# V in one transfer from ScalarE's queue, diagonal sums behind the masks, G's third band on VectorE: one planned attention-and-MLP kernel

## The chip, the cores and the metric

The kernel runs on 1 core of a Trainium2 chip. The metric is the device time of one execution in microseconds; the time before is 406.51 us, the median of 3 runs (405.24 to 407.18).

## The reference

Two stages, cut to what matters. Batch B is 4, heads H 8, positions S 768, head width D 48, model width 384, rank R 32, MLP width 1536.

```python
for t in range(S):
    cur = einsum('bhd,bhe->bhde', u * k[t], v[t])
    y[t] = einsum('bhd,bhde->bhe', r[t], state + cur)
    state = w * state + einsum('bhd,bhe->bhde', k[t], v[t])
x = y as (B, S, H * D)
xt = x.transpose(0, 2, 1)
u = x + (xt @ U @ V).transpose(0, 2, 1)
out = u + relu(u @ w_ch1) @ w_ch2
```

## The kernel before

**Attention in chunks.** Each batch's 768 positions are six chunks of 128 (`n` counts them over all batches; 0 to 5 are batch 0). A chunk's r, k and v come by DMA (`a_load`, L732, 192 KB each). TensorE turns r and k (`a_tr`, L849, tiles `ptr` and `ptk`); VectorE or ScalarE scales or copies the result (`rT` L858, `kT` L858 or L860). Scores go to `pab` (L881), updates of the running state to `pav` and `pst` (L895). VectorE masks the scores (`am`, L1018) and adds the state (`S`, L1057, L1059); ScalarE decays it for the next chunk (`SW`, L1067, four instructions). The chunk's output is summed in `pav` (L914, L918).

**The diagonal.** `a_dv` (L798) multiplies r by k on GpSimd, `a_dv_u` (L811) multiplies by u, `a_dg` (L818) sums over the head width on VectorE into `dg`, and ScalarE then multiplies v by `dg`, head by head, into `dv` (L822, eight instructions). `a_x` (L1027, VectorE) adds `dv` to the output sum and gives `x`. The next chunk's output sum may only begin when that read of `pav` is over.

**The low-rank step.** U and V, like the MLP weights, come as 64-bit words and are joined to 32 bits by ScalarE (L620, L633) and VectorE (L616, L623, L626). Six products with `x` (L1132) give G in three column groups of 32 rows. `c_g` writes G in three bands of rows: the rounded value (`high`, L1156, ScalarE), the rest (`low`, L1164, VectorE) and the rounded value again (`again_`, L1160, ScalarE). Then TensorE adds V times G to the turned x (`c_xu`, tiles `pu`, `uT`), and the MLP of batch 0 begins (`m_1`, `m_2`, L414). From there on TensorE interleaves the MLP of one batch with the attention of the next.

**What sets the order.** Every operation is recorded with a key (its rank) and a modelled duration; `Plan.schedule` then fixes the order on each engine, and the program is written in that order. Each engine, and each DMA queue, works through its list in order. SyncE (SP) issues nearly all DMAs. Each DMA signals one of eight semaphores, DMAHW0 to DMAHW7, in turn over all DMAs of the program, and a DMA that uses one of them again first waits until the earlier DMA of that semaphore has landed. The plan's model has no such wait.

**Lines that the change touches.** `unit` has `load`, which issues a weight's transfers (L595), and `weight_units` lists them; V is four transfers of 32 rows (L676), not a "big one" that counts among those in flight. `sel` (L1517) is the selection matrix with which `v_split` spreads V's pieces on TensorE. `prepare` records a chunk's diagonal sum of batch 0 (L1548) ahead of its visit, and `c_g` the bands.

Of the kernel before, what the change touches and what calls it, by code (L numbers as in the profile page):

```python
# [354 lines left out]
def rwkv_moe(ctx: ExitStack, tc: tile.TileContext, r, k, v, w, u, U, V, w1, w2, out):  # L355
    nc = tc.nc
# [51 lines left out]
    def f32(ap):  # L408
        return ap.bitcast(F32)
# [162 lines left out]
    def unit(name, shape, parts, split):  # L572

        P_ = shape[0]
        n = 1
        for s_ in shape[1:]:
            n *= s_
        raw = big([128, 2 * n], I32, f"raw_{name}") if wide else big([128, n], F32, f"raw_{name}")

        def view(ap):  # L580
            return ap if len(shape) == 2 else ap.rearrange("p (a c) -> p a c", a=shape[1])

        loaded = [(raw, i) for i in range(len(parts))]

        def load(mark=None):
            big_one = len(parts) == 1 and name != "u"
            before = landing[-FLYING] if big_one and len(landing) >= FLYING else None
            mine = []
            if big_one:
                landing.append((mine, Buf(const, [1, 1], F32, None, 1, f"landed_{name}")))  # L590
            for i, (p0, ap) in enumerate(parts):
                runs = 1 if len(ap.shape) == 2 else ap.shape[1]

                def start(q, p0=p0, ap=ap):
                    mine.append(q.dma_start(view(raw.t[p0:p0 + ap.shape[0]]), ap.bitcast(I32) if wide else ap))  # L595
                    if before:
                        tc.add_manual_dep(mine[0].ins, before[0][0].ins.name,
                                          mybir.DependencyInfo(mybir.DependencyClass.Sync, mybir.DependencyReason.DATA),
                                          reason="no more of them at a time")
                dma(start, [(raw, i)] + ([landing[-1][1]] if big_one else []), ([before[1]] if before else []) + ([mark] if mark else []),  # L600
                    ap.shape[0] * runs, (8 if wide else 4) * n // runs, ns=370, late=LATE + 1500 * (name == "v") + SLACK * (big_one and len(landing) <= 2 * EARLY))

        def word(i):
            return raw.t[:P_].rearrange("p (n two) -> p two n", two=2)[:, i]

        def byte():
            return raw.t[:P_].bitcast(U8).rearrange("p (n e) -> p n e", e=8)[:, :, 3]

        def fl():
            return view(word(0).bitcast(F32) if wide else raw.t[:P_])  # L610

        def on_dve_byte():
            return nc.vector.tensor_scalar(word(0), byte(), 2.0 ** -5, 7.0, ALU.mult, ALU.min)  # L616

        def on_act_byte():

            nc.scalar.activation(word(0), byte(), AF.Copy, scale=7.49 / 255)  # L620

        def sign():
            return nc.vector.scalar_tensor_tensor(word(0), word(1), -2 ** 31, word(0), ALU.bitwise_and, ALU.bitwise_or)  # L623

        def join():
            return nc.vector.scalar_tensor_tensor(word(0), word(1), 3, word(0), ALU.logical_shift_left, ALU.bitwise_or)  # L626

        def convert():
            if wide:
                op("DVE", 100 + 0.65 * n, on_dve_byte, [(raw, "lo")], loaded, lock=True,  # L630
                   alt=[("ACT", act(n) + 100, on_act_byte, False)])
            if wide:
                on_act(n, lambda: nc.scalar.activation(word(1).bitcast(F32), word(1).bitcast(F32), AF.Copy,  # L633
                                                       scale=2.0 ** -112), [(raw, "hi")], loaded)
                mark = [pool_done] if name in ALONE else []
                op("DVE", dve(n), sign, [(raw, "lo")], [(raw, "hi")] + mark, lock=True)
                op("DVE", dve(n), join, [(raw, "lo")], [(raw, "hi")], lock=True)
            split(fl, raw)
        return load, convert

    def weight_units():
        units = []

        def split_to(d, key, name):
            t = d[key] = big([128, 2, DM], F32R, name)

            def go(fl, raw):
                def to(i):
                    return t.t[:, i] if len(fl().shape) == 2 else t.t[:, i].rearrange("p (c n) -> p c n", c=NCT)
                on_act(384, lambda: nc.scalar.copy(to(0), fl()), [(t, 0)], [raw])  # L650
                on_either(384, lambda e: e.tensor_tensor(to(1), fl(), f32(to(0)), ALU.subtract), [(t, 1)],  # L651
                          [raw, (t, 0)], only=None)
            return go

        def u_split(fl, raw):
            on_act(192, lambda: nc.scalar.copy(Uf.t, fl()), [Uf], [raw])

        def v_split(fl, raw):
            for j in range(S // DM):
                pt = bank(("tr", "sc")[j], f"pv_{j}")  # L660

                def spread(j=j, pt=pt):
                    for i in range(DM // NV):
                        c = j * (DM // NV) + i
                        whole(pt.t[:3 * R, i * NV:(i + 1) * NV],
                              lhsT=sel.t[:, c * 3 * R:(c + 1) * 3 * R], rhs=fl(),
                              start=(i == 0), stop=(i == DM // NV - 1), skip_group_check=True)
                sl = slice(j * DM, (j + 1) * DM)
                pe(715, spread, [pt], [raw, sel], k=4)
                on_act(384, lambda sl=sl, pt=pt: nc.scalar.copy(V3.t[:, sl], pt.t[:3 * R, :DM]), [(V3, j)], [pt])  # L670
                on_dve(384, lambda e, sl=sl, pt=pt: e.tensor_tensor(V3.t[2 * R:, sl], pt.t[2 * R:3 * R, :DM],
                                                                    f32(V3.t[2 * R:, sl]), ALU.subtract), [(V3, j)], [pt])

        units.append(unit("u", [128, NCH, R], [(0, U.rearrange("(c p) r -> p c r", p=128))], u_split))
        NV = S * R // 128
        units.append(unit("v", [128, NV], [(c * R, V[:, c * NV:(c + 1) * NV]) for c in range(128 // R)], v_split))  # L676
        for f in range(NFT):
            fs = slice(f * 128, (f + 1) * 128)
            units.append(unit(f"w1_{f}", [128, NCT, 128], [(0, w1[:, fs].rearrange("(c p) n -> p c n", p=128))],
                              split_to(W1, f, f"w1s_{f}")))  # L680
            units.append(unit(f"w2_{f}", [128, DM], [(0, w2[fs, :])], split_to(W2, f, f"w2s_{f}")))
        return units
# [9 lines left out]
    def front(n):  # L692

        return n < NCH
# [444 lines left out]
    def c_g(b):  # L1139
# [8 lines left out]
        if not b:  # L1148
            G = Gs[b] = wbuf([3 * R, DM], F32R, "Gs", 1, f"Gs_{b}")

            def piece(g):
                return slice(g * 128, (g + 1) * 128), pt.t[g * R:(g + 1) * R, c0:c0 + 128]

            def high(g):
                c, p = piece(g)
                nc.scalar.copy(G.t[0:R, c], p)  # L1156

            def again_(g):
                c, _ = piece(g)
                nc.scalar.copy(G.t[2 * R:3 * R, c], f32(G.t[0:R, c]))  # L1160

            def low(e, g):
                c, p = piece(g)
                e.tensor_tensor(G.t[R:2 * R, c], p, f32(G.t[0:R, c]), ALU.subtract)  # L1164
            for g in range(NCT):
                on_act(128, lambda g=g: high(g), [(G, (0, g))], [pt])
            for g in range(NCT):
                on_dve(128, lambda e, g=g: low(e, g), [(G, (1, g))] + ([g_done] if g == NCT - 1 else []), [pt, (G, (0, g)), (G, (0, NCT - 1))])
            for g in range(NCT):
                on_act(128, lambda g=g: again_(g), [(G, (2, g))], [(G, (0, g))])  # L1170
            return
        gf = wbuf([R, DM], F32, "xl", NXS, f"gf_{b}")
        for g in range(4):
# [339 lines left out]
    for _ in range(START):  # L1513
# [2 lines left out]
    at(-99, lambda: a_load(0))  # L1516
    at(-98, lambda: on_act(384, lambda: nc.scalar.copy(  # L1517
        sel.t.rearrange("p (c k r) -> p c k r", k=3, r=R),
        ident_.rearrange("p (c r) -> p c r", r=R).unsqueeze(2).broadcast_to([128, 128 // R, 3, R])), [sel], []))
    at(UB, load_u)  # L1520
    at(-97, lambda: urgent(tables))
    for n in range(1, NCH):
# [18 lines left out]
    def prepare(n, t):  # L1541
# [3 lines left out]
        elif n < NCH:  # L1545
            fs = fs[1:2] + fs[3:4] + fs[2:3] + fs[:1] + fs[4:]
        fs.append(lambda: a_dv_u(n))
        if front(n):  # L1548
            fs.append(lambda: a_dg(n))
        for i, f in enumerate(fs):  # L1550
            at(t + (0.1 if n < NCH else 0.2) * i, (lambda f=f: urgent(f)) if n < NCH else lambda f=f: behind(u_done, f))

# [7 lines left out]
    def attention(b, t0, per, lead, step):  # L1560
        n0 = b * NCH
        end0 = t0 + per * NCH
        for c in range(NCH):
# [6 lines left out]
                    at(t - 2 * lead + 0.05 + 0.1 * i, lambda i=i: urgent(lambda: keep_busy(1 - i)))  # L1570
            if c == 0:
                at(t - 1, lambda n=n: urgent(lambda: a_first(n)) if b == 0 else a_first(n))
            at(t, lambda n=n: urgent(lambda: a_visit(n)) if b == 0 else a_visit(n))
            if n >= NCH:
                at(t - 0.1, lambda n=n: behind(u_done, lambda: a_dg(n)))
# [92 lines left out]
```

## Time and profile before

| | before |
|---|---|
| median of 3 runs (lowest to highest) | 406.51 us (405.24 to 407.18) |
| the three runs in order | 407.18, 406.51, 405.24 us |
| span of the profiled execution, first to last instruction | 406.6 us |
| TensorE, VectorE, ScalarE, GpSimd busy | 394.2, 274.8, 177.2, 65.4 us |
| TensorE's granted clock, mean over the span | 0.994 |

The profiled execution's own time is known as this span; it stands 0.1 us above the median of the runs. TensorE shows 97% of the span busy, but matmuls are pipelined and their ends modelled. What one edit is worth is read from its stage: the first 44.55 us are the attention of batch 0 and G, with waits; after them TensorE is busy almost without a break.

### The profile page before, as it was taken

The page shows a single profiled execution, that of the slowest core. Times are in us where ns is not written, and L with a number is a line of the kernel's source. Part 1 is how long each engine was busy: PE and PEld are TensorE (multiplying, and loading weights), DVE is VectorE, ACT ScalarE, POOL GpSimd, SP SyncE. Part 2 cuts the span into 40 slices and gives each one's busy share as a digit, 9 for nine tenths or more (in the row PEclk, how much of TensorE's full clock was granted, in tenths as well). Part 3 has the DMA queues.
Part 4 walks back from the last instruction along what each step waited for, and adds up shares of the span by engine and source line. Part 5 has one row for each costly group of instructions (what it writes and reads, how often), then busy time and mean ns, then how long its engine had stood idle before and what let it go on. Part 6 is the DMA issues. An engine that isn't in the chain of part 4 may idle for free.

```text
span 406.6 us, 11920 instructions
## 1 busy us (share of the span) xinstructions
PE 394.2 (97%) x4928; PEld 376.1 (92%) x4928; DVE 274.8 (68%) x615; ACT 177.2 (44%) x432; POOL 65.4 (16%) x86
## 2 busy tenths in 40 slices
PE   8997999999999999999999999999999999999994
PEld 5876899999998999999999999999999999999993
DVE  7868889999999979789647678898515261221122
ACT  2795859673786324223324242222224243223320
POOL 2960120233523302011003100010001000000000
PEclk9998999999999999999999999999999999999999
DMA  9969797968967765686667755782200520001001
GB/s 143 168 153 240 139 252 154 255 111 164 260 123 146 168 168 82 117 154 127 126 108 134 145 117 78 134 155 62 60 2 2 117 60 0 2 0 58 2 0 65
DMA packets 195741, 46.27 MB, mean 114 GB/s; under 512 B 179422, under 2 KB 194144, under 8 KB 195680
## 3 DMA queue, kind: packets, MB, share of 16 engines
q1 hardware_dynamic: 194352, 44.85, 55.2%
q8 instruction: 40, 0.66, 0.7%
q10 hardware_dynamic: 1328, 0.59, 0.5%
q14 instruction: 21, 0.17, 0.1%
HBM read 37.16 MB, written 8.26 MB: 112 GB/s over the span
## 4 chain that ended last, share of the span: by engine, by line
PE 75%; SPq 8%; DMA 5%; issue 4%; DVE 3%; POOL 2%; ACT 1%; DVEq 0%; POOLq 0%
PE p L414 64%; SPq L732 4%; PE pab L881 3%; SPq L771 2%; PE pav L932 2%; SPq L595 2%; PE pav L937 2%; PE pab L895 1%; DMA ub<-ud 1%; PE pab L414 1%; DMA ldr<-in_r_dram 1%; DMA ldv<-in_v_dram 1%; DMA vsw<-in_v_dram 1%; PE pav L914 1%; PE pav L918 1%
## 5 line engine op out<-in xcount | busy, mean ns | idle before, releaser
L414 PE MATMUL p<-uTh,w1s 128*128 128x384 f32 x576 | 147.6, 337 | 0.0
L1321 ACT ACTIVATE hr<-p 128x384 f32<-128x384 f32 x96 | 47.1, 491 | 178.0 <-PE p L414 173.7
L414 PE MATMUL p<-w2s,hh 128*128 128x384 f32 x576 | 119.6, 338 | 0.1
L1323 DVE TENSOR_TENSOR hl<-hr,hh 128x384 fp32r<-128x384 f32 x83 | 46.1, 555 | 102.3 <-ACT hh L1322 99.9
L414 PEld LDWEIGHTS p<-uTh,w1s 128*128 128x128 f32 x576 | 103.5, 188 | 0.9 <-DVE w1s L651 0.3
L414 PEld LDWEIGHTS p<-w2s,hh 128*128 128x128 f32 x576 | 100.7, 188 | 1.4 <-POOL w2s L651 0.4
L414 PE MATMUL p<-uTl,w1s 128*128 128x384 f32 x288 | 96.2, 335 | 0.0
L414 PE MATMUL p<-w2s,hl 128*128 128x384 f32 x288 | 66.7, 335 | 0.0
L414 PEld LDWEIGHTS p<-uTl,w1s 128*128 128x128 f32 x288 | 54.0, 188 | 0.1
L414 PEld LDWEIGHTS p<-w2s,hl 128*128 128x128 f32 x288 | 51.3, 188 | 0.2
L1322 ACT CAST hh<-hr 128x384 fp32r<-128x384 f32 x96 | 49.2, 512 | 2.5
L822 ACT ACTIVATE dv<-ldv,dg 128x48 f32<-128x48 f32 x96 | 23.1, 322 | 6.6 <-DVE dg L818 6.5
L1323 POOL TENSOR_TENSOR hl<-hr,hh 128x384 fp32r<-128x384 f32 x13 | 13.2, 1016 | 64.0 <-PE pav L937 36.7
L1095 POOL TENSOR_TENSOR SW<-S,wm 112x192 f32<-112x192 f32 x13 | 6.6, 508 | 93.2 <-DVE S L1086 87.8
L881 PEld LDWEIGHTS pab<-rT,kT 48*64 48x64 f32 x768 | 13.6, 134 | 7.7 <-issue 3.0
L1018 DVE TENSOR_TENSOR am<-pab,mask 128x256 f32<-128x256 f32 x48 | 19.1, 413 | 1.2 <-PE pab L881 1.1
L881 PE MATMUL pab<-rT,kT 48*64 48x64 f32 x768 | 16.9, 224 | 2.4 <-DVE rT L858 2.4
L1027 DVE TENSOR_TENSOR x<-pav,dv 128x384 f32<-128x384 f32 x24 | 13.1, 548 | 6.7 <-PE pav L937 5.2
L1361 DVE TENSOR_TENSOR x<-p,x 128x384 f32<-128x384 f32 x33 | 16.3, 548 | 1.0 <-PE p L414 1.0
L818 DVE TENSOR_REDUCE dg<-dv 128x8 f32<-128x384 f32 x24 | 13.0, 540 | 2.4 <-POOL dv L811 2.3
L626 DVE SCALAR_TENSOR_TENSOR raw_w<-raw_w 128x384 int32<-128x384 int32 x24 | 13.0, 549 | 0.1
L633 ACT ACTIVATE raw_w<-raw_w 128x384 f32<-128x384 f32 x24 | 13.0, 556 | 0.0
(178 smaller groups left out, 503.0 us busy)
## 6 DMA issues: line engine op xcount, KB each, us to landing
raw_w<-in_moe_w_ch_dram SPq DMA_DIRECT2D x24, 384.0 KB, 5.0
ldv<-in_v_dram SPq DMA_DIRECT2D x24, 192.0 KB, 3.9
ldk<-in_k_dram SPq DMA_DIRECT2D x20, 192.0 KB, 4.4
ldr<-in_r_dram SPq DMA_DIRECT2D x20, 192.0 KB, 4.0
bl<-in_r_dram SPq DMA_DIRECT2D x79, 48.0 KB, 3.1
bl<-in_k_dram SPq DMA_DIRECT2D x79, 48.0 KB, 2.4
ud<-x SPq DMA_DIRECT2D x18, 192.0 KB, 3.2
ub<-ud SPq DMA_DIRECT2D x18, 192.0 KB, 3.6
```

The lines of the kernel that those rows point to most:

```text
L414: return nc.tensor.matmul(*args, **kw)
L626: return nc.vector.scalar_tensor_tensor(word(0), word(1), 3, word(0), ALU.logical_shift_left, ALU.bitwise_or)
L633: on_act(n, lambda: nc.scalar.activation(word(1).bitcast(F32), word(1).bitcast(F32), AF.Copy, scale=2.0 ** -112), [(raw, "hi")], loaded)
L732: dma(lambda q, i=i, src=src: q.dma_start(part(i)[:, :, :D], src[b, :, c * C:(c + 1) * C, :].rearrange("h p d -> p h d")), [ts[i]] if n < ...
L822: nc.scalar.activation(dv.t[:, h], v_of(n, h), AF.Copy, scale=dg.t[:, h:h + 1])
L881: return nc.tensor.matmul(pt.t[o * C2:(o + 1) * C2, q * C2:(q + 1) * C2], lhsT=kT.t[rows, q, i * C2:(i + 1) * C2], rhs=rT.t[rows, q, i * C ...
L1018: on_dve(256, lambda e: e.tensor_tensor(am.t, abs_[n][j].t[:, :SU].rearrange("p (h t) -> p h t", h=NP), mask_.unsqueeze(1).broadcast_to([1 ...
L1027: nc.vector.tensor_tensor(x.t[:, c0:c1], pav[0].t[:, c0:c1], dv.t.rearrange("p h d -> p (h d)")[:, c0:c1], ALU.add)
L1321: on_act(384, lambda: nc.scalar.activation(hr.t, pt.t[:, :TB], AF.Relu), [hr], [pt])
L1322: on_act(384, lambda: nc.scalar.copy(hh.t, hr.t), [hh], [hr])
L1323: on_either(384, lambda e: e.tensor_tensor(hl.t, hr.t, f32(hh.t), ALU.subtract), [hl], [hr, hh], only=None)
L1361: on_dve(384, lambda e, x=x, pt=pt: e.tensor_tensor(x.t, pt.t[:, :DM], x.t, ALU.add), [x], [pt])
```

## The change

V is loaded by one transfer of 128 rows of 384 words, issued from ScalarE's queue, and `sel` selects every fourth row instead of a block of 32. Batch 0's diagonal sums are recorded just ahead of the chunk's visit, so that they rank behind the masks of that chunk. G's third band is copied by VectorE, group by group behind the second band, and the second band no longer names the last group of the first as what it waits for. V, now a single part, still isn't one of the big transfers that are counted in flight.

```diff
         def load(mark=None):
-            big_one = len(parts) == 1 and name != "u"
+            big_one = name not in ("u", "v")
...
-                    ap.shape[0] * runs, (8 if wide else 4) * n // runs, ns=370, late=LATE + 1500 * (name == "v") + SLACK * (big_one and len(landing) <= 2 * EARLY))
+                    ap.shape[0] * runs, (8 if wide else 4) * n // runs, ns=370, eng="ACT" if name == "v" else "SP", late=LATE + 1500 * (name == "v") + SLACK * (big_one and len(landing) <= 2 * EARLY))
...
-        units.append(unit("v", [128, NV], [(c * R, V[:, c * NV:(c + 1) * NV]) for c in range(128 // R)], v_split))
+        units.append(unit("v", [128, NV], [(0, V.rearrange("r (c n) -> (r c) n", n=NV))], v_split))
...
-            def again_(g):
+            def again_(e, g):
                 c, _ = piece(g)
-                nc.scalar.copy(G.t[2 * R:3 * R, c], f32(G.t[0:R, c]))
+                e.tensor_copy(G.t[2 * R:3 * R, c], f32(G.t[0:R, c]))
...
             for g in range(NCT):
                 on_act(128, lambda g=g: high(g), [(G, (0, g))], [pt])
-            for g in range(NCT):
-                on_dve(128, lambda e, g=g: low(e, g), [(G, (1, g))] + ([g_done] if g == NCT - 1 else []), [pt, (G, (0, g)), (G, (0, NCT - 1))])
-            for g in range(NCT):
-                on_act(128, lambda g=g: again_(g), [(G, (2, g))], [(G, (0, g))])
+                on_dve(128, lambda e, g=g: low(e, g), [(G, (1, g))] + ([g_done] if g == NCT - 1 else []), [pt, (G, (0, g))])
+                on_dve(128, lambda e, g=g: again_(e, g), [(G, (2, g))], [(G, (0, g))])
...
-        ident_.rearrange("p (c r) -> p c r", r=R).unsqueeze(2).broadcast_to([128, 128 // R, 3, R])), [sel], []))
+        ident_.rearrange("p (r c) -> p c r", r=R).unsqueeze(2).broadcast_to([128, 128 // R, 3, R])), [sel], []))
...
-        if front(n):
-            fs.append(lambda: a_dg(n))
...
+            if n < NCH:
+                at(t - 0.05, lambda n=n: urgent(lambda: a_dg(n)))
             at(t, lambda n=n: urgent(lambda: a_visit(n)) if b == 0 else a_visit(n))
```

In the order rows below a tile's number only tells two tiles of one name apart, and what stands behind "waits" are semaphores: of an engine, or DMAHWn of a DMA.

ScalarE's queue in chunks 0 and 1 (`dv_211` and `dv_278` or `dv_281` are the `dv` of chunks 0 and 1, `SW` the decayed state), before:

```order
L822 ACTIVATE dv_211<-ldv_112,dg_270 128x48 [waits DMAHW4_49,DVE_49]
L822 ACTIVATE dv_211<-ldv_112,dg_270 128x48 x7
L1067 ACTIVATE SW_325<-S_1_274,wm 112x96 [waits DVE_49]
L1067 ACTIVATE SW_325<-S_1_274,wm 112x96 x3
L822 ACTIVATE dv_278<-ldv_138,dg_344 128x48 [waits DMAHW7_49,DVE_49]
```

and now:

```order
L1067 ACTIVATE SW_276<-S_1_270,wm 112x96 [waits DVE_49]
L1067 ACTIVATE SW_276<-S_1_270,wm 112x96 x3
L595 DMA raw_v<-in_moe_V_dram 128x384 [waits DMAHW5_49]
L822 ACTIVATE dv_211<-ldv_112,dg_274 128x48 [waits DMAHW4_49,DVE_49]
L822 ACTIVATE dv_211<-ldv_112,dg_274 128x48 x7
L1067 ACTIVATE SW_360<-S_1_351,wm 112x96 [waits DVE_49]
```

The decay of chunk 0's state moved ahead of chunk 0's `dv`, and V's transfer stands between the two, with a wait for DMAHW5.

SP's queue in the change, around the load of chunk 3's v (`ldv_272`), the last DMA on DMAHW5 ahead of V's (each of these waits for the semaphore that it uses again):

```order
L732 DMA ld_128<-in_r_dram 128x8x48 [waits DMAHW4_49]
L732 DMA ldv_272<-in_v_dram 128x8x48 [waits DMAHW5_49]
L595 DMA raw_u<-in_moe_U_dram 128x6x64 [waits DMAHW6_49]
L732 DMA ldk_330<-in_k_dram 128x8x48 [waits DMAHW7_49]
L732 DMA ldr_120<-in_r_dram 128x8x48 [waits DMAHW0_49]
L732 DMA ldv_381<-in_v_dram 128x8x48 [waits DMAHW1_49]
L732 DMA ldk_419<-in_k_dram 128x8x48 [waits DMAHW2_49]
```

V's transfer waits until chunk 3's v has landed; chunk 5's k (`ldk_419`) now follows chunk 4's v (`ldv_381`) at once, where V's four transfers stood between them.

VectorE around chunk 0's x (`x_337`, now `x_358`), before:

```order
L1018 TENSOR_TENSOR am_1_323<-pab_108,mask 128x256 [waits PE_49]
L1027 TENSOR_TENSOR x_337<-pav_247,dv_211 128x384 [waits Activation_49]
L818 TENSOR_REDUCE dg_344<-dv_278 128x8 [waits Pool_49]
L1059 TENSOR_TENSOR S_0_349<-pav_90,SW_325 112x384 [waits PE_49,Activation_49]
L858 TENSOR_TENSOR kT_356<-ptk_242,tabT 112x512 [waits PE_49]
L1059 TENSOR_TENSOR S_1_388<-pst,S_0_349 112x384 [waits DVE_49]
```

and now:

```order
L1018 TENSOR_TENSOR am_1_324<-pab_108,mask 128x256 [waits PE_49]
L1059 TENSOR_TENSOR S_0_335<-pav_90,SW_276 112x384 [waits PE_49,Activation_49]
L858 TENSOR_TENSOR kT_344<-ptk_242,tabT 112x512 [waits PE_49]
L1059 TENSOR_TENSOR S_1_351<-pst,S_0_335 112x384 [waits DVE_49]
L1027 TENSOR_TENSOR x_358<-pav_247,dv_211 128x384 [waits Activation_49]
L858 TENSOR_TENSOR rT_383<-ptr_332,tabT 112x512 [waits PE_49]
L818 TENSOR_REDUCE dg_410<-dv_281 128x8 [waits Pool_49]
```

Chunk 0's x, which waits for ScalarE's `dv`, moved behind chunk 1's two state sums; chunk 2's `rT` and chunk 1's diagonal sum stand behind it.

## Rows read from the trace of the kernel before

**Rows 1.** Busy us of each engine by stage, granted clock, DMA share, GB/s.
```profile
0.00:44.55 44.55, 38.88 (x786) 31.22 (x786) 36.04 (x99) 27.99 (x97) 19.64 (x33) 0.96 0.96 178
44.55:100.00 55.45, 55.33 (x715) 53.11 (x714) 51.69 (x117) 39.16 (x93) 13.03 (x16) 1.00 0.82 181
```
**Rows 2.** The chain that ended last, in batch 0's attention: start us, us, what.
```profile
23.72 4.34 DMA ldr<-in_r_dram
...
29.34 0.97 POOL dv L811
...
40.60 0.60 PE wake L1132 x12
```
**Rows 3.** Timeline of VectorE, two places: start us, us, what [idle before, its releaser].
```profile
12.03 0.54 DVE L818 TENSOR_REDUCE dg<-dv 128x8 f32<-128x384 f32 x1
12.49 0.55 DVE L1059 TENSOR_TENSOR S<-pst,S 112x384 f32<-112x384 f32 x1
...
14.80 0.55 DVE L1027 TENSOR_TENSOR x<-pav,dv 128x384 f32<-128x384 f32 x1
...
30.33 0.55 DVE L818 TENSOR_REDUCE dg<-dv 128x8 f32<-128x384 f32 x1 [2.33 <-POOL dv L811]
```
**Rows 4.** Timeline of TensorE: chunk 5's scores.
```profile
32.75 0.69 PE L881 MATMUL pab<-rT,kT 48*64 48x64 f32 x32 [2.38 <-DVE rT L858]
```
**Rows 5.** Three stretches, columns of rows 1: chunk 0's x to chunk 5's scores, then outputs of chunks 4, 5.
```profile
14.80:32.75 17.95, 15.01 (x407) 12.72 (x405) 14.48 (x32) 16.74 (x65) 12.45 (x17) 1.00 0.78 181
33.45:36.50 3.05, 3.05 (x50) 2.73 (x49) 2.22 (x7) 1.20 (x3) 0.00 (x0) 0.50 1.05 216
37.80:39.75 1.95, 1.95 (x50) 1.78 (x49) 1.54 (x4) 0.92 (x2) 0.00 (x0) 1.00 1.06 155
```
**Rows 6.** Timeline of the queues of SP and ScalarE: DMA issues.
```profile
11.83 1.02 SPq L732 DMA_DIRECT2D ldv<-in_v_dram  x1
12.89 2.46 SPq L595 DMA_DIRECT2D raw_u<-in_moe_U_dram  x1
...
17.89 4.09 SPq L595 DMA_DIRECT2D raw_v<-in_moe_V_dram  x4
...
0.81 0.43 ACTq L732 DMA_DIRECT2D ld<-in_k_dram  x1
```
**Rows 7.** DMA issues at 10.45 and at 12.89: KB, us from issue to landing.
```profile
ld<-in_r_dram SPq DMA_DIRECT2D x1, 192.0 KB, 6.2
...
raw_u<-in_moe_U_dram SPq DMA_DIRECT2D x1, 192.0 KB, 5.2
```
**Rows 8.** Waits of SP's queue: us in total, times, longest us.
```profile
SPq L732 <- PE pab L849: 5.8, 3, 2.1
```
**Rows 9.** Timeline of ScalarE from chunk 0 to chunk 3.
```profile
12.61 1.92 ACT L822 ACTIVATE dv<-ldv,dg 128x48 f32<-128x48 f32 x8 [3.15 <-DVE dg L818]
14.43 1.16 ACT L1067 ACTIVATE SW<-S,wm 112x96 f32<-112x96 f32 x4
...
20.53 0.37 ACT L620 ACTIVATE raw_u<-raw_u 128x192 int32<-128x192 uint8 x1
20.80 0.36 ACT L633 ACTIVATE raw_u<-raw_u 128x192 f32<-128x192 f32 x1
21.07 0.56 ACT L860 COPY kT<-ptk 112x512 f32<-112x512 f32 x1
...
22.61 0.54 ACT L822 ACTIVATE dv<-ldv,dg 128x48 f32<-128x48 f32 x2
23.06 0.36 ACT L656 COPY Uf<-raw_u 128x192 f32<-128x192 f32 x1
23.32 1.46 ACT L822 ACTIVATE dv<-ldv,dg 128x48 f32<-128x48 f32 x6
```
**Rows 10.** Timeline of ScalarE and VectorE at G: third band, second band.
```profile
42.07 0.69 ACT L1160 CAST Gs<-Gs 32x128 fp32r<-32x128 f32 x3
...
42.76 0.92 DVE L1164 TENSOR_TENSOR Gs<-wake,Gs 32x128 fp32r<-32x128 f32 x3
```

## The prediction

> **What bounds the kernel now.** I read the busy time by stage first: from 44.55 us on TensorE stands still for 0.1 us in the 55 that follow, while up to 44.55 it is busy for 38.88 us only, at a mean clock of 0.96 [rows 1]. So what matters is when the first stage ends; whatever its last step, G, is late by, the end of the kernel is late by, one to one. I take that for every term below.
>
> The chain of waits then names what sets that stage's end: the load of chunk 5's r, landing at 28.06 (23.72 + 4.34), GpSimd's products for the diagonal up to 30.31, and, at its end, the products with x for G until 41.20 [rows 2]. VectorE's timeline says why GpSimd stands in that chain: a diagonal sum is in its queue ahead of work that is more urgent, and VectorE idles 2.33 us for it at 30.33 [rows 3]. TensorE's scores of chunk 5 come at 32.75 after 2.38 us of idling for VectorE's `rT` [rows 4]. What the idling costs beyond itself is in the windows: the granted clock then is 0.50 (1.2 GHz) and chunk 4's output takes 3.05 us, where chunk 5's, the same 50 matmuls, takes 1.95 at 2.4 GHz [rows 5]. That is 1.10 us; the scores and the G products on either side of it bring my estimate to 1.48 us for the whole half-clock stretch.
>
> **V's transfer on ScalarE.** SP gets rid of four issues that take 4.09 us [rows 6], so chunk 5's loads could come up to 4.1 us earlier. ScalarE gets one issue; its only load in this profile took 0.43 us there [rows 6]. But the order shows that this issue waits for a DMA semaphore, DMAHW5, last used by chunk 3's v, and that all of ScalarE's work, chunk 0's `dv` first, is queued behind it. That a queue can stand still like this is what SP's waits show: 5.8 us in three waits of up to 2.1 us [rows 8]. By the Trainium skill, "DMA: Bandwidth & Descriptors", section "Anatomy of one DMA — SWDGE (gpsimd) path", a semaphore wait is served by the issuing sequencer before the transfer is dispatched; the SP waits agree with it, and no row here shows it for ScalarE.
>
> When does chunk 3's v land? SP issues it at 11.83 [rows 6]. Its neighbour issued at 10.45 took 6.2 us, so landed at 16.65; U's, issued at 12.89, took 5.2 and landed at 18.09 [rows 7]. So v landed between the two; I take 17.4, the middle. ScalarE reaches the issue earlier. The diagonal sum, which VectorE did at 12.03 ahead of the state sum, now goes behind it, so the state sum is over at about 12.03 + 0.55 = 12.58 [rows 3]; `SW` takes 1.16 [rows 9] and ends near 13.8. Then ScalarE stands from 13.8 to 17.4, issues until 17.85, and runs chunk 0's `dv` (1.92 [rows 9]) until 19.77, where it now runs it at 12.61 to 14.53.
>
> Who waits for that: VectorE's `x` of chunk 0, at 14.80 now [rows 3], moves to about 19.85, and chunk 2's `rT` and chunk 1's diagonal sum are queued behind it. Chunk 1's output on TensorE waits for that `x` as well. TensorE will idle some 3 us there, and I expect its half-clock stretch there and not at chunk 4; it costs little, because ScalarE is later still.
>
> From chunk 0's `dv` on, ScalarE is the chain. Up to its copy of chunk 5's kT the new order gives it four `dv` (4 x 1.92), four `SW` (4 x 1.16), U's two joins (0.73), two `kT` (2 x 0.56), `Uf` (0.36), chunk 3's split `dv` (0.54 + 1.46) and two of chunk 5's (0.54): 17.07 us. Instructions overlap by about 0.10 (12.61 + 1.92 is 14.53, the next group begins at 14.43 [rows 9]); with 16 such hand-overs this is some 15.5. Waits add an estimated 1.2: 0.75 for chunk 1's diagonal sum behind the late `x`, and the rest for state sums and transposes. So the copy starts at 17.85 + 15.5 + 1.2 = 34.6, and is over at 35.2. VectorE is no later: from `x` to `rT` it has 14.48 us of work now [rows 5], less about 1.5 for the state sums and the `kT` that go ahead of `x`, plus 0.5 for U's join, as wide as a state sum: 19.85 + 13.5 = 33.3. So chunk 5's scores begin at about 35.2 in place of 32.75: **2.45 later**. The earlier loads are no use then, and the old wait for GpSimd is covered.
>
> From there to the end of the G products it is 41.20 − 32.75 = 8.45 us now; without the half-clock stretch (1.48) it is 6.95. So they end at 42.15: **+0.95 us**.
>
> **Diagonal sums behind the masks.** The same 96 `dv` and as many sums remain; nothing is added. The gain is the 2.33 us at 30.33 [rows 3], and it lies within the reckoning above: what is late next is ScalarE. With V on a queue that doesn't stall, this part would be the whole of the gain (rival 1).
>
> **G's third band.** VectorE's second band begins at 42.76, when ScalarE's third band, 0.69 us from 42.07, is over [rows 10]. So taking the third band off ScalarE shortens nothing by itself, and VectorE gets three more instructions. A copy of that shape costs ScalarE 0.23 (0.69/3), VectorE's second band 0.31 (0.92/3) [rows 10]; I take 0.31, the engine's own, for +0.92 at most. Against it, one weight join as wide as a state sum (0.55 [rows 3], some 0.47 with its overlap) that now stands ahead of the second band goes behind, and VectorE may begin as soon as the first group is rounded, not the last, for which I take another 0.25 off. Net **+0.2**, with ends of −0.5 and +0.9.
>
> **Selection.** `sel` is the same number of elements from another stride, once, long before it is needed: 0; its cover is the whole of the attention stage.
>
> **Sum.** 406.6 + 0.95 + 0.2 = **407.8 us**. The span of 406.6 stands 0.1 above the median of the runs, so nothing is added for that. This case's own range, by the landing (16.65 to 18.09, −0.75 to +0.7) and G's ends, is 406.3 to 409.2. Half a per cent, 2.0 us, is about what a measurement of this kernel can tell from no change; so this case is "same".
>
> **Rival 1: ScalarE doesn't stall.** If the landing is no condition when ScalarE comes to the issue, or the wait is held by the queue and not by the engine, `dv` begins at 13.8 + 0.43 = 14.25, `x` of chunk 0 at about 16.3, and the copy of kT ends at 14.25 + 15.5 + 1.2 + 0.55 = 31.5. Scores begin 1.3 earlier than now, the half-clock stretch is gone (1.48), G adds 0.2: 404.0. For it speaks the 0.43 us of the k load [rows 6], which nothing held up; against it that this load was ScalarE's first, with no semaphore to use again, and that SP is held by such waits [rows 8]. Chance 0.2. The Trainium skill, same page, section "Issuing engines are not separate DMA queues", says that issuing from several engines saves only the sequencer's issue time; by it the loads can gain at most the 4.09 us that SP loses, and no bandwidth, which leaves this rival at 404.0.
>
> **Rival 2, slower: the issue is expensive.** V's transfer may cost its queue what the 192 KB of U cost SP, 2.46 us [rows 6], in place of 0.43. All of it falls on ScalarE's chain: +2.0, 409.8. From 0.85 us more on that chain than I reckon the kernel is slower by 2.0, so an issue above 1.3 us decides for it. U has six runs to a row where V has one, which speaks against it; chunk loads of eight runs took 1.02 on SP [rows 6] and 0.43 on ScalarE. Chance 0.15.
>
> **Rival 3, slower: the half clock comes back.** If TensorE, with ScalarE pacing it, idles some 2.4 us ahead of chunk 5's scores as it does now [rows 4], the 1.48 us isn't given back: 409.3. Against it: the delay lies at chunk 1, and TensorE has 15.01 us of work in the 17.95 before the scores [rows 5], so the rest of its idle time should come in pieces. Chance 0.15.
>
> **How the numbers follow.** The forecast has 0.5, rival 1 0.2, rivals 2 and 3 0.15 each. Faster is rival 1: 0.2; slower are rivals 2 and 3: 0.3; same the rest: 0.5. The range reaches from rival 1 with a little of its own spread, 403.8, to rival 2, 410.0.
>
> **What would show it.** ScalarE idle from about 13.8, with V's issue at about 17.4 and chunk 0's `dv` at 17.9; `x` of chunk 0 near 19.85 with a long idle ahead of it; the clock low at chunk 1 and not at chunk 4; scores of chunk 5 near 35; G's products ending near 42.1; six alternating small VectorE instructions at G; chunk 5's r landing near 24. I am wrong if `dv` of chunk 0 begins by 14.5 (rival 1), if the issue itself takes over a microsecond (rival 2), or if the clock is 0.50 after the scores of chunk 5 (rival 3).

## The result and the profile after

| | before | after |
|---|---|---|
| median of the runs | 406.43 us (4 runs, 405.24 to 407.18) | 411.27 us (4 runs, 410.72 to 412.23) |
| ratio, 95% interval | | 1.0117 [1.0074, 1.016] |
| span of the profiled execution | 406.6 us | 409.6 us |
| TensorE's mean granted clock in it | 0.994 | 0.991 |

The kernel became 4.8 us slower. That is above the range (410.0 at most), on the side to which I had given 0.3.

The busy time by stage of the kernel after (from:to, us, then PE, PEld, DVE, ACT, POOL busy with their counts, clock, DMA share, GB/s):

```profile
0.00:44.55 44.55, 38.50 (x774) 31.00 (x774) 33.68 (x92) 26.73 (x90) 19.61 (x33) 0.92 0.96 183
44.55:100.00 55.45, 53.40 (x658) 50.95 (x657) 51.02 (x117) 39.05 (x92) 10.69 (x13) 1.00 0.75 164
20.15:26.55 6.40, 6.36 (x110) 5.60 (x114) 4.25 (x10) 4.32 (x17) 2.82 (x4) 0.50 0.76 167
```

Beside [rows 1]: in the first 44.55 us ScalarE was busy for 1.3 us less (26.73 against 27.99), the clock is 0.92, and there is a stretch of 6.4 us at 0.50. ScalarE's timeline, from chunk 0 on:

```profile
12.62 1.17 ACT L1067 ACTIVATE SW<-S,wm 112x96 f32<-112x96 f32 x4 [3.16 <-DVE S L1059]
17.18 0.36 ACTq L595 DMA_DIRECT2D raw_v<-in_moe_V_dram  x1
17.64 1.91 ACT L822 ACTIVATE dv<-ldv,dg 128x48 f32<-128x48 f32 x8 [3.85 <-DMA ldv<-in_v_dram]
...
21.23 1.91 ACT L822 ACTIVATE dv<-ldv,dg 128x48 f32<-128x48 f32 x8 [0.62 <-DVE dg L818]
...
26.19 0.58 ACT L860 COPY kT<-ptk 112x512 f32<-112x512 f32 x1 [1.46 <-PE ptk L849]
```

ScalarE is done with the decay at 13.79 and idles 3.85 us; V's issue comes at 17.18 and takes 0.36; chunk 0's `dv` begins at 17.64 instead of 12.61 [rows 9]. The row names a load of v as what ended the idling. It is chunk 3's v, for which V's issue waits: SP issued it at 11.93, and it landed 5.2 us later, at 17.13, 0.05 us before V's issue began.

```profile
11.93 2.27 SPq L732 DMA_DIRECT2D ldv<-in_v_dram  x1
```

The last of ScalarE's rows is a second wait, of 1.46 us, for transposes of TensorE (chunk 3's k). VectorE's timeline:

```profile
19.58 0.56 DVE L1027 TENSOR_TENSOR x<-pav,dv 128x384 f32<-128x384 f32 x1 [3.06 <-ACT dv L822]
...
41.92 0.55 DVE L651 TENSOR_TENSOR w1s<-raw_w,w1s 128x384 fp32r<-128x384 f32 x1
42.50 0.56 DVE L1027 TENSOR_TENSOR x<-pav,dv 128x384 f32<-128x384 f32 x1
...
44.61 0.28 DVE L1164 TENSOR_TENSOR Gs<-wake,Gs 32x128 fp32r<-32x128 f32 x1
44.92 0.22 DVE L1160 CAST Gs<-Gs 32x128 fp32r<-32x128 f32 x1
```

Chunk 0's `x` is at 19.58 instead of 14.80 [rows 3]; chunk 5's is at 42.50, behind a weight's split; the third band of G alternates with the second, and each of its copies takes 0.22. TensorE's two longest waits (us in total, times, longest), and its scores of chunk 5, the last six products with x and the first MLP product:

```profile
PE pav L914 <- DVE x L1027: 2.5, 1, 2.5
PE pab L881 <- ACT kT L860: 0.7, 1, 0.7
```

```profile
36.17 0.69 PE L881 MATMUL pab<-rT,kT 48*64 48x64 f32 x32 [0.67 <-ACT kT L860]
...
43.12 0.42 PE L1132 MATMUL wake<-x,Uf 128*32 128x128 f32 x6 [0.25 <-DVE x L1027]
...
46.93 0.59 PE L414 MATMUL p<-uTh,w1s 128*128 128x384 f32 x2
```

The scores come 3.42 us later than at 32.75 [rows 4], the first MLP product 2.38 later than at 44.55, where the second stage of [rows 1] begins. From there to the end it is 362.7 us, before it was 362.05.

### The profile page after: what moved, and what is told of

It is laid out like the page before. It is cut to its first block, busy times and chain, and to the rows that moved or that the text cites. A ratio compares the mean times of both kernels' runs of the same rounds, so it can differ in the third digit from the quotient of the medians.

```text
span 409.6 us, 11920 instructions
## 1 busy us (share of the span) xinstructions
PE 395.6 (97%) x4926; PEld 377.0 (92%) x4926; DVE 273.7 (67%) x616; ACT 183.2 (45%) x453; POOL 65.5 (16%) x84
## 4 chain that ended last, share of the span: by engine, by line
PE 65%; DVE 3%; SPq 1%; DMA 1%; issue 0%; ACT 0%; DVEq 0%; ACTq 0%
PE p L414 58%; PE pab L881 2%; PE pav L932 1%; PE pav L937 1%; PE pab L895 1%; PE pab L414 1%; SPq L771 1%; PE pab L1132 1%; DMA bl<-in_k_dram 1%; DVE raw_w L626 0%; DVE rT L840 0%; DVE hl L1321 0%; DVE raw_w L623 0%; DVE w2s L651 0%; DVE x L1359 0%
## 5 line engine op out<-in xcount | busy, mean ns | idle before, releaser
L1321 DVE TENSOR_TENSOR hl<-hr,hh 128x384 fp32r<-128x384 f32 x88 | 48.9, 555 | 102.0 <-ACT hh L1320 100.2
L822 ACT ACTIVATE dv<-ldv,dg 128x48 f32<-128x48 f32 x112 | 26.9, 322 | 11.2 <-DVE dg L818 6.2
L1321 POOL TENSOR_TENSOR hl<-hr,hh 128x384 fp32r<-128x384 f32 x8 | 8.1, 1016 | 64.8 <-PE pav L937 39.1
L1095 POOL TENSOR_TENSOR SW<-S,wm 112x192 f32<-112x192 f32 x11 | 5.6, 507 | 70.8 <-DVE S L1086 64.6
L811 POOL TENSOR_TENSOR dv<-dv,ub 128x384 f32<-128x384 f32 x11 | 11.1, 1006 | 13.6 <-DVE raw_u L626 5.4
```

Source lines behind the costliest of these rows:

```text
L811: on_either(384, lambda e: e.tensor_mul(dv.t, dv.t, ub.t), [dv] + ([pool_done] if n == NCH - 1 else []), [ub], only="POOL" if front(n) els ...
L822: nc.scalar.activation(dv.t[:, h], v_of(n, h), AF.Copy, scale=dg.t[:, h:h + 1])
L1321: on_either(384, lambda e: e.tensor_tensor(hl.t, hr.t, f32(hh.t), ALU.subtract), [hl], [hr, hh], only=None)
```

## The experiments

A run's time is some 1.7 us above its span: the four of the kernel after are 411.32, 412.23, 410.72 and 411.22 us at spans of 409.6, 410.5, 409.0 and 409.5. The kernel before ran beside each set: 405.79 us (26 runs) with the first four rows, 405.64 (17) with the next four, 405.11 (24) with the last three; the ratios are against these. "First MLP" is the start of the first MLP product in the profiled execution.

| run | median us | ratio [95%] | first MLP |
|---|---|---|---|
| V on SP, rest as changed | 407.5 | 1.0040 [1.0022, 1.0057] | 47.47 |
| V alone changed | 411.51 | 1.0153 [1.0130, 1.0175] | 47.65 |
| diagonal sums alone | 406.87 | 1.0028 [1.0009, 1.0046] | 42.90 |
| G's third band alone | 406.0 | 1.0014 [0.9987, 1.0040] | 41.63 |
| before, profiled again | 405.67 (1 run) | | 41.51 |
| changed, with filler | 410.35 | 1.0121 [1.0084, 1.0157] | 48.56 |
| changed, V later on ScalarE | 406.9 | 1.0033 [1.0013, 1.0052] | 42.82 |
| V on SP, weights held | 408.73 | 1.0083 [1.0052, 1.0114] | 42.47 |
| V on SP, stall put back | 410.51 | 1.0123 [1.0089, 1.0157] | 46.90 |
| before, one V transfer on SP | 407.97 | 1.0063 [1.0042, 1.0085] | 41.69 |
| before, V later on ScalarE | 404.72 | 0.9988 [0.9970, 1.0007] | 41.97 |

**One part at a time.** The first takes the changed kernel and issues V from SP:

```diff
-                    ... ns=370, eng="ACT" if name == "v" else "SP", late=LATE + 1500 * (name == "v") ...
+                    ... ns=370, late=LATE + 1500 * (name == "v") ...
```

> The changed kernel with one part undone: V stays one transfer of 128 rows, but SP issues it. Theory (ScalarE standing behind V's issue until chunk 3's v has landed is the loss): ScalarE has dv of chunk 0 begun by 14.5 us, chunk 0's x is near 16.3, no half clock at chunk 1, chunk 5's scores near 31.5, and the kernel takes about 404 us (402.5 to 405.5), some 7 us less than the changed one. Rival A (the late diagonal sums are the loss): 409 to 411. Rival B (G's third band on VectorE): 409 to 411, with chunk 5's scores early but the first MLP product late.

The next three apply one part of the change's diff to the kernel before: V's transfer with its queue, the two places of `a_dg`, the bands of G.

> Only V's transfer is changed: one transfer from ScalarE's queue, which now stands in the middle of chunk 0's eight dv; the diagonal sums and G stay as before. Theory: ScalarE stands at the issue for some 3 us until about 17.2, chunk 0's x comes near 19, the clock falls to 1.2 GHz behind it, and the kernel takes 409 to 412 us. Rivals A and B: the stall is absorbed, 405 to 407 us.

> Only the diagonal sums of batch 0 go behind the masks; V is four transfers from SP, G as before. Theory: ScalarE never stands still for it, the idling of VectorE for GpSimd at 30.3 us goes, half a clock or not as TensorE's idle time falls, and the kernel takes 403 to 406 us. Rival A: 409 to 411 us, dv and with it x are late in every chunk.

> Only G's third band goes to VectorE. Theory: 406 to 407 us (from -0.5 to +0.9 against the kernel before). Rival B: 408 to 411 us, with the first MLP product 2 us later than in the kernel before.

V's transfer alone costs as much as the whole change. ScalarE in that run, where the issue falls among chunk 0's eight `dv`:

```profile
12.62 1.01 ACT L822 ACTIVATE dv<-ldv,dg 128x48 f32<-128x48 f32 x4 [3.15 <-DVE dg L818]
17.30 0.35 ACTq L595 DMA_DIRECT2D raw_v<-in_moe_V_dram  x1
17.69 1.01 ACT L822 ACTIVATE dv<-ldv,dg 128x48 f32<-128x48 f32 x4 [4.07 <-DMA ldv<-in_v_dram]
```

G costs nothing that can be told. (The profiled execution with V on SP, 411.22 us, is the second slowest of 11, of which nine took 408.0 or less; from 32 to 42 us its clock is 0.51, so its first MLP product at 47.47 is no usual one.) With V on SP the stall and most of the loss go (`dv` begins at 13.69), but the kernel isn't at 404 as the theory said: 407.5 is above the kernel before, and the diagonal sums alone cost 1.1 us where a gain was expected. So a second theory was needed for what had looked like the gain.

**Was the profile of before a usual execution?**

> The kernel before, profiled once more. Theory: the half clock at chunk 4 in its first profile is not in every execution; in this one the clock stays at 1.00 from 12 us on, chunk 5's scores come near 31.2, the first MLP product near 41.7 and the span is 403 to 405 us. Rival: it is part of the kernel's course, the clock falls to 0.50 near 33 us again and the span is 406 to 407 us.

It was not a usual one. The busy time by stage and, below, TensorE's timeline of this second profile:

```profile
0.00:44.55 44.55, 40.32 (x803) 32.58 (x804) 38.86 (x106) 30.75 (x104) 19.64 (x33) 1.00 0.95 181
```

```profile
30.98 0.69 PE L881 MATMUL pab<-rT,kT 48*64 48x64 f32 x32 [0.33 <-ACT kT L860]
...
41.51 0.78 PE L414 MATMUL p<-uTh,w1s 128*128 128x384 f32 x3
```

The clock is 1.00 over the stage, the scores wait 0.33 us instead of 2.38 [rows 4], and the first MLP product comes 3.04 us earlier than in the first profile. With those 1.7 us the first profile's execution took some 408.3, more than any of the four runs in the table above; of the 72 other timed executions of the kernel before, two took longer. Against the second profile the change costs 5.42 us up to the first MLP product, of 5.6 in the span: the loss lies in front of the MLP. SP's issues differ as well: V's four take 2.18 us in the second profile, where the first has 4.09 [rows 6].

**Is it the stall?** Two runs, from both sides. The first leaves V on ScalarE and lets it wait for the same load of chunk 3, but records it with the marks of the first weights, so that it stands behind chunk 2's `dv`:

```diff
-        at((U_LOAD, V_LOAD)[i] if i < 2 else ...
+        at((U_LOAD, FRONT + EACH * HOLD)[i] if i < 2 else ...
```

> The changed kernel with V's transfer still one of ScalarE's queue and still with the same wait for chunk 3's v, but in the queue behind chunk 2's dv, when that load has long landed. Theory (the stall at the issue is the loss, not the queue or the engine): no idling of ScalarE at the issue, the kernel takes 406.5 to 408.5 us, as with V on SP. Rival (a transfer from ScalarE's queue costs in itself, by its issue or by landing late): 410 to 412 us.

The second has V on SP and makes chunk 0's first `dv` wait for chunk 3's v without need (`landed` holds the loads' instructions):

```diff
+                if n == 0 and h == 0:
+                    tc.add_manual_dep(one.ins, landed[3, 2].ins.name, ..., reason="stall")
```

> The changed kernel with V on SP, as in the first experiment, but the first instruction of chunk 0's dv on ScalarE waits for the landing of chunk 3's v, which it doesn't need: the stall without the transfer. Theory (the stall is the loss): ScalarE idles from 13.8 to about 17.2, TensorE runs at 1.2 GHz from 20 us, and the kernel takes 410.5 to 412.5 us. Rival (what the transfer does on ScalarE's queue adds a part): 408 to 410 us.

ScalarE with V's issue later, then with the stall alone (line numbers 1 higher), and the window of the latter. In the program V stands behind chunk 2's `dv`, which begins at 22.02; the row of its issue is earlier, at 21.26, so in this trace an issue on ScalarE's queue runs ahead of work of the engine that is queued before it:

```profile
13.85 1.90 ACT L822 ACTIVATE dv<-ldv,dg 128x48 f32<-128x48 f32 x8
...
21.26 0.40 ACTq L595 DMA_DIRECT2D raw_v<-in_moe_V_dram  x1
...
22.02 1.92 ACT L822 ACTIVATE dv<-ldv,dg 128x48 f32<-128x48 f32 x8
```

```profile
17.60 1.91 ACT L823 ACTIVATE dv<-ldv,dg 128x48 f32<-128x48 f32 x8 [3.81 <-DMA ldv<-in_v_dram]
```

```profile
20.15:26.55 6.40, 6.39 (x110) 5.63 (x114) 4.25 (x10) 4.33 (x17) 2.81 (x4) 0.50 0.91 228
```

The same transfer from the same queue shows no stall where its wait is over, and the kernel takes 406.9 us; the wait without the transfer in that queue gives 410.51 us, the same 6.4 us at 0.50 and the first MLP product at 46.90, where the changed kernel has 46.93. So the stall is most of the loss: with it the ratios are 1.0117 and 1.0123, without it 1.0040 and 1.0033. What is left without it, 0.3 to 0.4 per cent, is about what the diagonal sums alone cost (1.0028).

**What does the low clock add?** 17 idle products go ahead of chunk 1's output, in the same recorded operation:

```diff
-  ... lambda: in_turn(*mine), [pav[0]], own, ...
+  ... lambda: ([fill() for _ in range(17 if n == 1 else 0)], in_turn(*mine)), [pav[0]], own, ...
```

> The changed kernel with 17 idle products of 128x128 (about 2.4 us) on TensorE between chunk 1's updates and chunk 1's output, where it stands for chunk 0's x. ScalarE stalls as before. Theory now: the half clock from 20 to 26.5 us is a price of its own, by making TensorE late for ScalarE's kT of chunk 3; with the products the clock stays at 1.00, chunk 5's scores come 1 to 2 us earlier (34 to 35.2) and the kernel takes 409 to 410.3 us. Rival (my prediction: ScalarE binds anyway): the clock stays up but scores come at 36 and the kernel takes 411 to 412 us.

Windows of the run, then ScalarE's kT of chunk 3:

```profile
17.60:20.20 2.60, 2.60 (x28) 2.60 (x24) 0.43 (x1) 2.38 (x11) 2.52 (x4) 1.00 1.15 258
20.20:26.55 6.35, 6.33 (x165) 5.64 (x164) 4.92 (x12) 5.70 (x23) 2.79 (x4) 1.00 0.89 200
33.00:36.60 3.60, 3.09 (x24) 2.70 (x24) 0.87 (x3) 1.73 (x7) 0.20 (x1) 0.57 0.78 158
```

```profile
24.99 0.59 ACT L860 COPY kT<-ptk 112x512 f32<-112x512 f32 x1
```

With the filler the clock stays at 1.00, ScalarE doesn't wait for the transposes, and its kT is at 24.99 instead of 26.19: 1.2 us earlier, though `dv` began 0.18 later. In this profiled execution (411.84 us, the second slowest of six) the clock fell later, at 33, behind another idling of TensorE of 1.8 us, so its scores of chunk 5 say nothing. The median is 0.9 below the changed kernel's, but against the kernel before that ran beside it the ratio is 1.0121, no better than 1.0117, and the spread, 409.06 to 413.37, is wide: the 1.2 us on ScalarE's chain are shown in one profile, a gain in time is not.

**Why are the diagonal sums no gain?** TensorE's longest wait in the kernel with the sums alone, and in that with V on SP ("issue" means that the profile shows nothing that it waited for):

```profile
PE pav L895 <- issue: 1.5, 1, 1.5
```

```profile
PE pav L895 <- issue: 2.5, 1, 2.5
```

Instruction transfers of the latter on queue q8 between 30 and 33 us (packets, MB, share of the DMA engines):

```profile
q8 instruction: 1, 0.02, 3.0%
```

Between 25 and 30 us there is none on that queue; the trace doesn't say for which engine they are. In the second profile of before one starts at 27.76, and TensorE waits 0.3 us at that place. Four more profiles are in line: it starts at 28.2 with one V transfer on SP and the old sums (wait 1.0, which the profile puts down to VectorE's mask), at 28.9 with V later on ScalarE in the changed kernel (wait 1.2), at 29.5 with the sums alone (1.5) and at 30.1 with V on SP (2.5). I took it that TensorE stood there for its own instructions, held up by the weights' packets. So, with V on SP, the first weights were held:

```diff
-    SPLIT, HOLD = 5, 2
+    SPLIT, HOLD = 5, 3
...
+                    if name == "w1_0":
+                        tc.add_manual_dep(mine[0].ins, am_ins[3].ins.name, ..., reason="the weights later")
```

> The changed kernel with V on SP and with the first MLP weights' transfers held until VectorE has masked chunk 3's scores (some 3 us later). Theory: with V on SP TensorE stood 2.5 us at chunk 4's updates for its own instructions, whose transfer came behind the weights' packets; held back, the instruction transfer starts near 26.4 and not near 30, TensorE doesn't stand there, chunk 5's scores come near 31.3, and the kernel takes 405 to 406.5 us. Rival (TensorE waits there for something of the kernel, or the weights are then late themselves): the idling stays or moves behind, 407 to 409 us.

The instruction transfers on q8 between 25 and 30 us, then TensorE's longest wait (line numbers are 5 higher here):

```profile
q8 instruction: 1, 0.02, 2.3%
```

```profile
PE pab L886 <- ACT kT L865: 1.0, 1, 1.0
```

The transfer is early (26.85) and the wait at the updates is gone; but the six runs went from 406.92 (the profiled one) to 410.32, and the median, 408.73, is no better than with V on SP and lies where the rival had it. That the wait goes with a late instruction transfer fits these six profiles; that it is the cause of the 1.1 us isn't shown, and that stays open.

**V as one transfer without the stall.**

> The kernel before with V as one transfer of 128 rows, still from SP. Theory: in a usual execution the loads of chunk 5 are not what TensorE waits for, so SP's freed time is worth nothing: 405 to 406.3 us. Rival (my prediction's chain: SP's four issues delay the front): 403 to 404.5 us.

> The kernel before with V as one transfer from ScalarE's queue, behind chunk 3's dv, where it waits for no semaphore. Theory: as the one transfer on SP, 405 to 406.5 us, against 411.5 with the same transfer ahead of chunk 0's last four dv. Rival: ScalarE's queue or V's late landing costs, 407.5 us or more.

The edit of the second is that of V later on ScalarE, on the kernel before; there V stands behind chunk 3's `dv` in the program, and its issue is at 22.70. It measures as the kernel before does (0.9970 to 1.0007), so no version here beats it for certain. On SP the one transfer cost 1.7 to 3.4 us, and neither the theory nor the rival of its run had that. SP's issue of it, 2.11 us:

```profile
17.93 2.11 SPq L595 DMA_DIRECT2D raw_v<-in_moe_V_dram  x1
```

Its profiled execution (406.96 us, below the median) has the first MLP product at 41.69, near the 41.51 of before: there the loss lies later. I don't know its cause. The long issue need not be it: the same transfer took SP 0.77 to 1.03 us in the three runs with V on SP.

## Why the prediction was wrong

Two steps failed: the half clock at chunk 1, which the prediction put at almost nothing, and the baseline, a span taken for a time and an odd execution for a usual one. The stall itself was forecast well.

- **The stall: right.** Issue at 17.18 (17.4 forecast), 0.36 us (0.43), `dv` at 17.64 (17.85), `x` of chunk 0 at 19.58 (19.85), low clock at chunk 1 and no longer at chunk 4, chunk 5's r landing at 25.1 (near 24). Two runs show that it is most of the loss.
- **"It costs little, because ScalarE is later still": wrong.** At 1.2 GHz TensorE was so late with chunk 3's transposes that ScalarE waited for them 1.46 us. I had 1.2 us for all of ScalarE's waits, of which 0.75 for chunk 1's sum (0.62 measured); the two waits make 2.08. Scores of chunk 5: 36.17 in place of 35.2, +0.97.
- **From the scores to the last product with x, 6.95 us: too short.** It took 7.37 (36.17 to 43.54), +0.42. Of this 0.25 is TensorE's wait for chunk 5's `x`, which stood behind a weight's split on VectorE until 42.50. (8.45 − 1.48 is 6.97 and not 6.95; this changes nothing.)
- **G, +0.2: 0.04.** From the end of those products to the first MLP product it took 3.39 us, before 3.35 (44.55 − 41.20 [rows 2]); alone 1.0014 [0.9987, 1.004].
- **"Late one to one": nearly.** The rest of the kernel took 0.62 us more; over all profiles here that rest varies from 361.0 to 363.5 us, so this is no term that can be named.
- **"The span stands 0.1 above the median, so nothing is added": the larger failure.** Some 1.7 us lie outside the span of each run. The forecast of 407.75 was a span; as a time it was 409.5. The measured span is 409.6, which is 1.85 off, and the steps above add up to that: 0.97 + 0.42 − 0.16 + 0.62.
- **The credit of 1.48 us for a half-clock stretch given back, and the 2.33 us of VectorE at 30.33: not there in a usual execution.** They belonged to an execution of 408.3 us. The second profile has neither. Hence +4.8 us against the median, where the two profiled executions differ by 3.0: the first profile's execution took 1.9 us more than the median with which it was equated. The 4.09 us that SP was to save are no constant either: 2.18 in the second profile.
- **Rival 1, 404.0 without the stall: wrong that it beats the kernel before.** Without the stall the kernel takes 407.5 us on SP and 406.9 later on ScalarE: faster than the changed kernel, slower than the kernel before. The rival took its gain from those two stretches, and its 404.0 was a span too, so 405.7 as a time. **Rival 2** is out: the issue took 0.36 us. **Rival 3** had a price for the low clock, but in the wrong place: it didn't return at chunk 4, and it wasn't free at chunk 1.
- **The rule that issuing from several engines saves only the sequencer's time** (the Trainium skill, "DMA: Bandwidth & Descriptors", "Issuing engines are not separate DMA queues") isn't contradicted by the two runs that have V later on ScalarE: SP is rid of V's issues, and the ratios of 1.0033 and 0.9988 show no gain. **That a semaphore wait is served by the issuing sequencer** (the Trainium skill, same page, "Anatomy of one DMA — SWDGE (gpsimd) path") is now seen on ScalarE too, which stood for 3.85 us.

## What to carry to other kernels

A transfer moved to a compute engine's queue brings its semaphore's wait along, and everything behind it in that queue waits too: look up which earlier load holds that semaphore and put the issue where that load has landed. Before a stretch of a profile is credited as a gain, compare the profiled execution's own time, with what lies around its span (here 1.7 us), with the other runs: an odd execution offers gains that the usual one doesn't have. A stall of another engine is not free for TensorE even if TensorE isn't the bound: at the clock that it then gets it can become the bound, as here, where ScalarE waited 1.46 us for it.

## What the runs showed that I had not expected

- After 2.55 us without work TensorE ran at 0.50 for 6.4 us, though it was busy for 6.36 of them; with filler in the gap it stayed at 1.00.
- The same 192 KB transfer of 128 rows took 0.35 to 0.40 us to issue on ScalarE (five kernels, four places in its queue) and 0.77 to 2.11 on SP (four kernels).
- Two executions of one program, the kernel before, differ by 3.04 us at the first MLP product.
